# A written-out schedule of a fused attention and token-mixing kernel, laid out once more behind the first scores

## The chip, the cores and the metric

The kernel runs on one core of one Trainium2 chip. The metric is the device time of one execution in microseconds (us); the times of several executions are given as their median. The core has five engines that run side by side, each through its own instructions in a fixed order: PE (TensorE, matrix products; its weight loads are shown as PEld), DVE (VectorE), ACT (ScalarE), POOL (GpSimd) and SP (SyncE, which issues transfers). Transfers (DMAs) are issued by GpSimd, SP or ACT, and run in queues behind them on 16 DMA engines. An engine that needs another's result waits on a semaphore, and everything behind the waiting instruction on that engine waits too.

## What is computed

Two attentions one behind the other, for 8 batches, 8 heads, 576 tokens and a head size of 64, and then a token mixer over the 8 batches.

```python
def sm_attn(qq, kk, vv):
    s = scale * np.matmul(qq, kk.transpose(0, 1, 3, 2))
    s = s - np.max(s, axis=-1, keepdims=True)
    a = np.exp(s)
    a = a / (np.sum(a, axis=-1, keepdims=True) + 1e-09)
    return np.matmul(a, vv)
p_packed = sm_attn(p, k, v)               # 32 packed rows per head
out = sm_attn(q, p_packed, p_packed)      # 576 rows per head
...
x = out.transpose(0, 2, 1, 3).reshape(B, S, H * D)
wq = x @ w_q
wk = x @ w_k
W_tok = scale * np.einsum('bsd,btd->bst', wq, wk)
mixed = np.einsum('bst,btd->bsd', W_tok, x)
return (np.maximum(mixed, 0.0) @ w_out)
```

The inputs q, k and v are 8 x 8 x 576 x 64 in float32, the output is 8 x 576 x 512 in float32. The products run in bfloat16.

## The kernel before

The whole program is one list, the string ORDER, of some 520 items in a fixed order, with engine and banks written out. A loop at the end of the kernel takes the items one after the other and emits the instructions of each. An item reads `STEP.batch.part=banks@engine`: `PV.0.0=4,5` is the step PV of batch 0, part 0, with its result in PSUM banks 4 and 5, and `AE.0.2@A` is a step that runs on ACT (V is DVE, P is GpSimd; a store without a letter goes out by SP). Steps that are matrix products have no letter, since they run on PE. So the order of the list is the order of the instructions on each engine; between engines only the data and the buffers decide.

The steps of one batch b, in the order in which they depend on each other, with the lines under which the profile shows them:

- Loads: LD.k, LD.v, LD.q (L175, L172, L181; halves of q: LD.q7 and LD.r7, L178) by GpSimd's queue, cast from float32 to bfloat16 on the way. LD.O is the output weight, LD.N and LD.W are p and the two small weights (by ACT and SP).
- KT and QV (L236): transposes of k and of q on DVE, in blocks of 32 x 32.
- First attention: S1 (L281), scores of p with k; X1 (L292, ACT), their exponential; TE (L236, DVE), its transpose; PV (L314), the product with v, in which a column of ones gives the sum; RC (L318) and PP (L322) on DVE, the division; PT (L236, DVE), the transpose of the packed rows.
- Weights folded in: QK (L335), the packed rows times w_k and w_q; QKE, its copy out of PSUM (L127 on ACT, L131 on DVE); QD (L129, GpSimd), a second copy of a part.
- Second attention: S2 (L372), scores of q; X2 (L377, ACT), the exponential; RS (L393) and RR (L398) on DVE, sum and reciprocal (for batch 5 HA, L387, adds halves on GpSimd first); AM (L404, mostly GpSimd), the multiplication; AT (L413 and L418), the transpose on PE; AE (L127 or L131), its copy out of PSUM. Part 2 of S2, AM and AT is the last quarter of 256 elements, part 3 the four other token tiles (1,024 elements); in batches 0, 1 and 7 these are two parts, 0 and 1.
- Mixer: WKQ (L440, L445) and its copy WE; GM (L466) and GE; Y (L476) and YE (L483 on ACT, L485 on DVE); MX (L491) and MR (L497), the mixed rows; RL, RLF and RLR (L502 on ACT, L504 on DVE), the ReLU; OT (L539), the product with w_out, five tiles of 128 tokens (OT.b.4 for a pair of batches together); OE and OEF (L127 or L131), the copy out of PSUM; ST (L558, L560) and STF (L589), the stores. The last tile of batch 7 is done in halves: OH (L576), OEH and STH (L585).

WARM.n (L614) is a product of a constant buffer with itself, n times 128 columns, whose result nobody reads; it keeps PE at work while it would wait. HOLD.v7 (L571) is a tiny transfer by SP that reads v of batch 7: SP, whose stores stand behind it, goes no further until that load has landed.

The loads run in the order of the batches: k0, v0, q0, k1, k2, v1, q1, v2, q2, O, k3, v3, k4, q3, v4, q4, k5, v5, q5, k6, v6, q6, k7, and then the last ones. Input buffers are four deep, most others two or three, the result buffer o six (batch 6 writes where batch 0 lay, batch 7 where batch 1 lay). PE works on several batches at a time: while the first attention of one batch is on its way through ACT and DVE, PE does S2, WKQ or OT of an earlier one.

Of the kernel before, what the change touches and what calls it, by code (L numbers as in the profile page):

```python
# [13 lines left out]
LD.g0 LD.v0 LD.r0 LD.q0 LD.k1 NC.0@V PX.0@V NC.1@A PX.1@V SET.aff@P SET.idb@V SET.v3@P KT.0.0@V SET.mask@P  # L14
WC.1@P WC.0@P LD.k2 SET.v1@P LD.v1 SET.v2@P KT.0.1@V WARM.4=0 WARM.22.128=0 S1.0=0,1,2,3 X1.0.1@A TE.0.1@V
X1.0.0@A TE.0.0@V WARM.8=4 PV.0.0=4,5 PV.0.1 RC.0@V PP.0.0@V PP.0.1@V LD.q1 PT.0@V WARM.6=6 QK.0=6 QKE.0@A
QV.0.0@V QV.0.1@V QD.0@P WARM.4=7 S2.0.2=2,3 X2.0.2@A RS.0.2@V RR.0.2@V S2.0.0=0,1 LD.v2 S2.0.1=4,5 X2.0.0@A
RS.0.0@V RR.0.0@V X2.0.1@A RS.0.1@V RR.0.1@V AM.0.2@P WARM.6=7 AT.0.2=7 AE.0.2@A AM.0.0@P WARM.5=6 AT.0.0=6
KT.1.2@V AM.0.1@P WARM.3=2 AT.0.1=7 AE.0.1@A AE.0.0@V WKQ.0.0=2,3 WKQ.0.2 WE.0.0@A LD.q2 WKQ.0.1 KT.2.2@V
S1.1=0,1,4,5 WE.0.1@A GM.0=6 X1.1.0@A TE.1.0@V GE.0@A WARM.2=7 Y.0=2,3 YE.0@V S1.2=0,1,6,7 MR.0=2,3 X1.1.1@A  # L20
TE.1.1@V MX.0.0=4,5 X1.2.0@A LD.O PV.1.0=0,1 TE.2.0@V PV.1.1 X1.2.1@A TE.2.1@V RC.1@V LD.k3 PP.1.0@V PP.1.1@V
PT.1@V MX.0.1=6,7 QV.1.2@V RLR.0@A QK.1=2 QKE.1@V RL.0.0@A WARM.3=3 S2.1.2=4,5 S2.1.0=0,1 RL.0.1@A X2.1.2@A
RS.1.2@V RR.1.2@V S2.1.1=2,3 X2.1.0@A RS.1.0@V RR.1.0@V WARM.1=6 PV.2.0=6,7 PV.2.1 X2.1.1@A RS.1.1@V RC.2@V
LD.v3 QD.1@P AM.1.2@P AT.1.2=4 RR.1.1@V AM.1.0@P WARM.5=5 AT.1.0=5 AM.1.1@P LD.k4 PP.2.0@V AE.1.2@A PP.2.1@V
PT.2@V QK.2=4 AE.1.0@A QKE.2@A QD.2@P QV.2.2@V LD.q3 LD.v4 AT.1.1=0 AE.1.1@A WKQ.1.0=2,3 WKQ.1.2 WKQ.1.1
WE.1.0@V S2.2.2=6,7 WE.1.1@A X2.2.2@A S2.2.3=4,5 X2.2.3@A GM.1=1 OT.0.0=2,3 GE.1@V Y.1=6,7 OT.0.1 YE.1@A
RS.2.4@V OE.0.0@A MR.1=0,1 MX.1.1=4,5 RLR.1@A RR.2.4@V OT.0.2=6,7 LD.q4 OT.0.3 KT.3.2@V AM.2.3@P OE.0.1@V
RL.1.1@A S1.3=2,3,0,1 X1.3.0@A AM.2.2@P OT.1.4=4 TE.3.0@V LD.k5 AT.2.2=5 X1.3.1@A TE.3.1@V AT.2.3=2 AE.2.3@V
LD.v5 MX.1.0=6,7 AE.2.2@V PV.3.0=0,1 PV.3.1 OEF.1.4@A WKQ.2.0=2,3 WKQ.2.1 RC.3@V PP.3.1@V RL.1.0@A WKQ.2.2
WE.2.2@A OT.1.2=4,5 OT.1.3 PP.3.0@V PT.3@V QK.3=6 OE.1.1@A LD.q5 KT.4.2@V S1.4=0,1,2,3 GM.2=7 OT.1.0=4,5  # L30
X1.4.1@A LD.k6 GE.2@A QKE.3@V X1.4.0@A QV.3.2@V TE.4.1@V Y.2=2,3 YE.2@A S2.3.2=6,7 X2.3.2@A S2.3.3=0,1
X2.3.3@A MX.2.0=2,3 TE.4.0@V RL.2.0@A MR.2=6,7 RLR.2@V OT.1.1 MX.2.1=6,7 RL.2.1@A OE.1.0@A PV.4.0=0,1 QD.3@P
PV.4.1 RS.3.4@V RR.3.4@V LD.v6 AM.3.3@P AM.3.2@P RC.4@V OT.2.0=2,3 OT.2.1 LD.q6 OE.2.0@A PP.4.0@V PP.4.1@V
PT.4@V QK.4=6 AT.3.3=7 QV.4.2@V AT.3.2=0 AE.3.2@A LD.k7 S2.4.2=4,5 AE.3.3@V X2.4.2@A S2.4.3=2,3 X2.4.3@A
KT.5.2@V WKQ.3.0=0,1 WKQ.3.1 WKQ.3.2 RS.4.4@V RR.4.4@V QKE.4@A WE.3.2@A S1.5=4,5,2,3 X1.5.1@A LD.v7 TE.5.1@V
OT.2.2=6,7 AM.4.3@P QD.4@P AM.4.2@P GM.3=0 X1.5.0@A TE.5.0@V GE.3@A OT.2.3 Y.3=2,3 YE.3@V PV.5.0=4,5 PV.5.1
HOLD.v7 MR.3=0,1 RC.5@V PP.5.1@V OE.2.1@A MX.3.0=2,3 PP.5.0@V PT.5@V MX.3.1=6,7 RLR.3@A RL.3.0@A OT.3.4=0
RL.3.1@A AT.4.2=1 AE.4.2@A OEF.3.4@A QV.5.2@V AT.4.3=5 AE.4.3@V ST.1.4@P QK.5=4 QKE.5@V QD.5@P S2.5.2=2,3
X2.5.2@A KT.6.2@V S2.5.3=6,7 X2.5.3@A HA.5@P WKQ.4.0=0,1 WKQ.4.2 LD.q7 WKQ.4.1 WE.4.2@A OT.3.0=2,3
S1.6=4,5,6,7 X1.6.0@A GM.4=0 GE.4@V TE.6.0@V LD.r7 OT.3.1 X1.6.1@A TE.6.1@V Y.4=0,1 OE.3.0@A RS.5.4@V RR.5.4@V  # L40
PV.6.0=4,5 YE.4@A PV.6.1 MX.4.0=6,7 RC.6@V RL.4.0@A PP.6.0@V AM.5.3@P PP.6.1@V PT.6@V MX.4.1=2,3 AM.5.2@P
OT.3.2=0,1 OT.3.3 RL.4.1@A QK.6=4 QKE.6@A QV.6.2@V ST.2.1 S2.6.2=6,7 X2.6.2@A S2.6.3=2,3 ST.3.4 MR.4=4,5
# [5 lines left out]
OEF.5.4@A S2.7.1=6,7 ST.5.4 ST.1.0 GM.6=3 GE.6@V X2.7.1@A RS.7.1@V RR.7.1@V S2.7.2=0,1 X2.7.2@A S2.7.0=4,5
QK.7=2 X2.7.0@A RS.7.0@V RR.7.0@V Y.6=6,7 YE.6@A OT.5.2=0,1 MX.6.1=4,5 QKE.7@A MX.6.0=6,7 AM.7.1@P RS.7.2@V
RR.7.2@V MR.6=2,3 OT.5.3 RLR.6@V RL.6.0@V RL.6.1@A OE.5.1@A ST.4.1 AM.7.0@P OT.5.0=2,3 AM.7.2@P AT.7.0=4  # L50
AE.7.0@A AT.7.1=5 AE.7.1@V AT.7.2=6 AE.7.2@V OT.6.2=0,1 OEF.6.2@A QD.7@P WKQ.7.0=4,5 WKQ.7.2 WKQ.7.1 WE.7.0@A
WE.7.1@A STF.6.2 OT.6.0=6,7 OT.6.1 GM.7=0 OE.6.0@V OT.5.1 OE.5.0@V ST.5.1@P GE.7@A Y.7=4,5 OT.6.3 OEF.6.3@V
ST.6.0 STF.6.3 YE.7@A ST.5.0 MR.7=6,7 RLR.7@A MX.7.0=4,5 RLF.7.0.1@A RLF.7.0.0@V MX.7.1=2,3 RLF.7.1.0@A
OT.7.4=0 OEF.7.4@A ST.7.4 RLF.7.1.1@V OT.7.1=6 OEF.7.1@V OT.7.0=7 STF.7.1 OT.7.2=1 OEF.7.0@A OH.7.0=0 STF.7.0
OEF.7.2@A STF.7.2 OEH.7.0@V STH.7.0 OH.7.1=5 OEH.7.1@A STH.7.1@A
"""


# [589 lines left out]
```

## Time and profile before

| What | us |
|---|---|
| median of 3 executions | 104.16 |
| lowest and highest | 104.09 and 104.93 |
| the profiled execution | 104.06 |
| its span from the first instruction to the last | 102.2 |

The page of the profile gives for each engine how much of the span it was busy: PE 92.8 us (91%), DVE 73.5 us (72%), ACT 65.1 us (64%), GpSimd 53.3 us (52%). Its line of slices cuts the span into 40 equal parts of 2.56 us; GB/s counts the bytes that the DMA engines moved, where a load counts with its bfloat16 size. A row of the timeline gives start and length in us, the engine, the line, the operation, the output and the inputs by the program's names, the number of instructions merged into it (x2), and in brackets how long the engine had been idle and what ended that. Of products the length reaches to the end of the last one's tail, so that the next row of PE may begin before it.

### The profile page before, as it was taken

What the parts mean: (1) busy time and instruction counts of PE and PEld (TensorE: products, weight loads), DVE (VectorE), ACT (ScalarE), POOL (GpSimd) and SP (SyncE); (2) the same over time, 40 slices, a digit from 0 to 9 for tenths busy, and PEclk for the clock granted to TensorE, in tenths of its full rate; (3) what the DMA queues carried; (4) which work ended last, traced back from release to release, by engine and by line L of the source; (5) the groups of instructions that cost most, each with busy time, mean ns of one, the idle gap of its engine ahead of it and who ended that gap; (6) DMA issues with size and microseconds to landing.
All of it is one profiled execution on the core that took longest, in us unless ns stands there. A gap on an engine that the chain in (4) does not pass through costs nothing.

```text
span 102.2 us, 3594 instructions
## 1 busy us (share of the span) xinstructions
PE 92.8 (91%) x1536; PEld 54.6 (53%) x1536; DVE 73.5 (72%) x140; ACT 65.1 (64%) x111; POOL 53.3 (52%) x83
## 2 busy tenths in 40 slices
...
DMA  1999999999999999999999999999999999997894
GB/s 25 257 233 208 213 211 215 204 213 208 207 208 209 212 208 212 214 208 208 213 208 208 214 211 206 214 210 211 249 249 391 410 418 408 417 389 281 330 368 153
DMA packets 13567, 25.13 MB, mean 246 GB/s; under 512 B 1072, under 2 KB 6448, under 8 KB 13552
## 3 DMA queue, kind: packets, MB, share of 16 engines
...
q10 hardware_dynamic: 560, 0.52, 1.9%
...
HBM read 30.15 MB, written 9.44 MB: 387 GB/s over the span
## 4 chain that ended last, share of the span: by engine, by line
PE 50%; DMA 21%; DVE 8%; POOL 7%; ACT 7%; issue 3%; SPq 1%; POOLq 0%; DVEq 0%; ACTq 0%
PE ps L539 26%; DMA q_sb<-in_q_dram 13%; DMA o<-in_moe_w_q_dram 8%; PE ps L372 4%; POOL a L404 4%; PE ps L314 3%; ACT e1T L292 3%; PE ps L418 3%; PE ps L445 3%; DVE rs L393 2%; PE ps L440 2%; PE ps L466 2%; PE ps L281 2%; ACT e L377 1%; DVE qT L236 1%
## 5 line engine op out<-in xcount | busy, mean ns | idle before, releaser
L539 PE MATMUL ps<-wout,relu 128*128 128x512 bf16 x124 | 30.6, 380 | 0.0
L404 POOL TENSOR_TENSOR a<-e,rr 128x256 bf16<-128x256 f32 (+2 forms) x18 | 19.5, 1098 | 16.9 <-DVE rr L398 6.4
L614 PE MATMUL ps<-o 128*128 128x128 f32 (+3 forms) x76 | 19.3, 398 | 1.2 <-DVE o L134 1.2
L539 PEld LDWEIGHTS <-relu 128*128 128x128 bf16 x124 | 10.7, 98 | 11.7 <-issue 1.1
L127 ACT ACTIVATE o<-ps 128x1024 f32<-128x1024 f32 (+2 forms) x13 | 11.4, 878 | 5.4 <-PE ps L539 5.2
L614 PEld LDWEIGHTS ps<-o 128*128 128x128 f32 x76 | 11.2, 206 | 5.3 <-issue 3.6
L502 ACT ACTIVATE relu<-ps 128x1024 bf16<-128x1024 f32 (+1 forms) x14 | 12.9, 967 | 1.1 <-PE ps L491 1.1
L292 ACT ACTIVATE e1T<-ps 128x576 bf16<-128x576 f32 x16 | 9.8, 655 | 5.3 <-PE ps L281 4.7
L377 ACT ACTIVATE e<-ps 128x256 f32<-128x256 f32 (+2 forms) x19 | 11.2, 622 | 2.8 <-PE ps L372 2.6
L393 DVE TENSOR_REDUCE rs<-e 128x16 f32<-128x512 f32 (+2 forms) x13 | 10.9, 841 | 2.3 <-ACT e L377 2.2
L236 DVE STREAM_TRANSPOSE kT<-k_sb 128x1152 uint32<-128x1152 uint32 (+1 forms) x9 | 11.0, 1226 | 2.0 <-DMA k_sb<-in_k_dram 2.0
L172 POOL DMA_DIRECT2D v_sb<-in_v_dram x16 | 10.0, 629 | 4.6 <-DMA v_sb<-in_v_dram 1.4
L236 DVE STREAM_TRANSPOSE qT<-q_sb 128x1152 uint32<-128x1152 uint32 (+1 forms) x10 | 11.0, 1112 | 0.4 <-DMA q_sb<-in_q_dram 0.2
L131 DVE COPY o<-ps 128x1024 f32<-128x1024 f32 (+2 forms) x7 | 6.6, 958 | 5.0 <-PE ps L539 2.7
L236 DVE STREAM_TRANSPOSE e<-e1T 128x288 uint32<-128x288 uint32 x16 | 7.4, 469 | 2.5 <-ACT e1T L292 2.0
L127 ACT ACTIVATE aT<-ps 128x128 bf16<-128x128 f32 (+2 forms) x11 | 5.0, 465 | 5.7 <-PE ps L418 3.3
L314 PE MATMUL ps<-v_sb,e 64*64 64x192 bf16 x288 | 7.7, 245 | 0.8 <-DVE e L236 0.5
L127 ACT ACTIVATE wkq<-ps 128x448 bf16<-128x448 f32 (+1 forms) x10 | 7.2, 729 | 1.8 <-PE ps L445 1.7
L314 PEld LDWEIGHTS <-e 64*64 64x64 bf16 x288 | 6.0, 107 | 2.7 <-DVE e L236 2.0
L372 PEld LDWEIGHTS <-qT 64*128 64x128 bf16 x320 | 5.4, 94 | 2.8 <-DVE qT L236 1.8
L372 PE MATMUL ps<-ppT,qT 64*128 64x64 bf16 x320 | 6.6, 190 | 0.3 <-DVE qT L236 0.2
L445 PE MATMUL ps<-aT,pqk 128*128 128x256 bf16 (+1 forms) x48 | 6.8, 246 | 0.0
...
## 6 DMA issues: line engine op xcount, KB each, us to landing
...
```

The source lines that it names most:

```text
L127: nc.scalar.activation(o, i, COPY)
L172: nc.gpsimd.dma_start(v_bufs[b % NL][halves(i), 0:7:2], src)
L236: nc.vector.transpose(o, i)
L292: nc.scalar.activation(e1T[:, x], T["s1", b][x].rearrange("a c m -> a m c"), EXP, scale=scale)
L314: nc.tensor.matmul(T["pv", b][halves(cc), i], lhsT, rhs, start=n == 0, stop=n == R - 1, skip_group_check=True)
L372: nc.tensor.matmul(ps[:, y, t - t0, i], lhsT, rhs, start=e == 0, stop=e == 1)
L377: nc.scalar.activation(e2[:, t0:t1].rearrange("a t (i y n) -> a y (t i) n", i=2, y=2), T["s2", b, c].rearrange("a y t i n -> a y (t i) n") ...
L393: nc.vector.tensor_reduce(rs[:, t0 * H:t1 * H], src, axis=AX, op=ADD)
L404: e.tensor_tensor(a2[:, t0:t1].rearrange("a t i (u l) -> a (t i u) l", l=L), e2v(b, c), T["rr", b][:, t0 * H:t1 * H].to_broadcast((P, (t1 ...
L502: nc.scalar.activation(o, i, RELU)
L539: nc.tensor.matmul(ps, lhsT, wout[:, j, :], start=j == 0, stop=j == NJ - 1)
L614: nc.tensor.matmul(bank(int(bk), [w]), warm[:, 0:P], rhs, start=True, stop=True)
```

## The change

Nothing but the string ORDER is changed, from its second line on. Up to the first scores (S1.0) only LD.k2 and setup steps of GpSimd and KT.0.1 change place; the steps behind them are laid out once more: their order, the banks of their results, and for 28 steps the engine. Every load, product and store of the old list stands in the new one; the WARM items differ (69 units of 128 columns before, 79 after). Of the loads, q7 comes ahead of v7; it was between v7 and r7.

For the steps that the prediction speaks of, by engine, with the old order under the minus sign and the new one under the plus sign:

```diff
 PE, from the first wait for q of batch 1
-QK.1 WARM.3 S2.1.2 S2.1.0 S2.1.1 WARM.1 PV.2.0 PV.2.1 AT.1.2 WARM.5 AT.1.0 QK.2 AT.1.1 WKQ.1.0 WKQ.1.2 WKQ.1.1 S2.2.2 S2.2.3 GM.1
-OT.0.0 Y.1 OT.0.1 MR.1 MX.1.1 OT.0.2 OT.0.3 S1.3 OT.1.4 AT.2.2 AT.2.3 MX.1.0 PV.3.0 PV.3.1 WKQ.2.0 WKQ.2.1 WKQ.2.2 OT.1.2 OT.1.3
-QK.3 S1.4 GM.2 OT.1.0 Y.2 S2.3.2 S2.3.3 MX.2.0 MR.2 OT.1.1 MX.2.1 PV.4.0 PV.4.1 OT.2.0 OT.2.1 QK.4 AT.3.3 AT.3.2 S2.4.2 S2.4.3
+WARM.1 QK.1 WARM.7 S2.1.2 S2.1.0 S2.1.1 WARM.4 PV.2.0 PV.2.1 AT.1.2 WARM.4 AT.1.0 QK.2 WKQ.1.0 WKQ.1.2 AT.1.1 S2.2.2 S2.2.3 WKQ.1.1
+OT.0.2 OT.0.3 GM.1 OT.0.0 OT.0.1 Y.1 S1.3 MR.1 AT.2.2 AT.2.3 MX.1.0 MX.1.1 PV.3.0 PV.3.1 WKQ.2.0 WKQ.2.2 WKQ.2.1 OT.1.2 OT.1.3
+GM.2 QK.3 S1.4 Y.2 OT.1.4 MX.2.1 S2.3.2 S2.3.3 OT.1.0 MR.2 MX.2.0 PV.4.0 PV.4.1 OT.1.1 OT.2.0 OT.2.1 QK.4 AT.3.3 AT.3.2 S2.4.2 S2.4.3
...
 PE, batch 5
-PV.5.0 PV.5.1 MR.3 MX.3.0 MX.3.1 OT.3.4 AT.4.2 AT.4.3 QK.5 S2.5.2 S2.5.3 WKQ.4.0 WKQ.4.2 WKQ.4.1 OT.3.0 S1.6 GM.4 OT.3.1 Y.4 PV.6.0
+PV.5.0 PV.5.1 AT.4.2 MR.3 MX.3.0 MX.3.1 OT.3.4 AT.4.3 S2.5.2 S2.5.3 WKQ.4.0 WKQ.4.1 WKQ.4.2 OT.3.0 S1.6 GM.4 OT.3.1 QK.5 Y.4 PV.6.0
...
 PE, the end
-AT.7.0 AT.7.1 AT.7.2 OT.6.2 WKQ.7.0 WKQ.7.2 WKQ.7.1 OT.6.0 OT.6.1 GM.7 OT.5.1 Y.7 OT.6.3 MR.7 MX.7.0 MX.7.1 OT.7.4 OT.7.1 OT.7.0 OT.7.2 OH.7.0 OH.7.1
+AT.7.1 AT.7.2 OT.5.1 AT.7.0 OT.6.2 WKQ.7.0 WKQ.7.1 WKQ.7.2 OT.6.0 GM.7 OT.6.1 Y.7 OT.6.3 MR.7 MX.7.0 MX.7.1 OT.7.4 OT.7.2 OT.7.1 OT.7.0 OH.7.1 OH.7.0
 DVE, batches 1 to 2
-RS.1.0 RR.1.0 RS.1.1 RC.2 RR.1.1 PP.2.0 PP.2.1 PT.2 QV.2.2 WE.1.0 GE.1 RS.2.4 RR.2.4 KT.3.2 OE.0.1 TE.3.0
+RS.1.0 RR.1.0 RS.1.1 RC.2 PP.2.1 PP.2.0 PT.2 RR.1.1 AE.1.0 QV.2.2 RS.2.4 RR.2.4 KT.3.2 YE.1 RLR.1 TE.3.1
 DVE, batches 3 to 5
-PT.3 KT.4.2 QKE.3 QV.3.2 TE.4.1 TE.4.0 RLR.2 RS.3.4 RR.3.4 RC.4 PP.4.0 PP.4.1 PT.4 QV.4.2 AE.3.3 KT.5.2 RS.4.4 RR.4.4
-TE.5.1 TE.5.0 YE.3 RC.5 PP.5.1 PP.5.0 PT.5 QV.5.2 AE.4.3 QKE.5 KT.6.2
+PT.3 KT.4.2 GE.2 QKE.3 QV.3.2 TE.4.0 RL.2.1 TE.4.1 RS.3.4 RR.3.4 RC.4 PP.4.0 PP.4.1 PT.4 QV.4.2 QKE.4 AE.3.3 KT.5.2 RS.4.4 RR.4.4
+TE.5.0 TE.5.1 YE.3 RC.5 PP.5.0 PP.5.1 QV.5.2 PT.5 AE.4.3 KT.6.2
 DVE, batch 7
-AM.6.3 TE.7.1 TE.7.0 QV.7.1 AE.6.3 QV.7.0 RC.7 PP.7.0 PP.7.1 PT.7 RL.5.0 GE.6
+AM.6.3 TE.7.0 GE.5 TE.7.1 QV.7.1 AE.6.3 AE.6.2 RC.7 QV.7.0 PP.7.0 PP.7.1 PT.7 RL.5.0 GE.6
 GpSimd, from the AM steps of batch 2, and its stores
-LD.q4 AM.2.3 AM.2.2 LD.k5
+LD.q4 AM.2.2 AM.2.3 LD.k5
...
-LD.q6 LD.k7 LD.v7 AM.4.3 QD.4 AM.4.2 ST.1.4 QD.5 HA.5 LD.q7 LD.r7 AM.5.3 AM.5.2 ST.1.1 ST.0.1 ST.3.0 AM.6.2 QD.6 AM.7.1 AM.7.0 AM.7.2 QD.7 ST.5.1
+LD.q6 LD.k7 LD.q7 AM.4.2 QD.4 AM.4.3 LD.v7 HA.5 ST.1.4 LD.r7 AM.5.2 AM.5.3 ST.3.0 QD.5 ST.3.4 ST.0.1 QD.6 ST.1.1 AM.6.2 AM.7.1 AM.7.2 AM.7.0 QD.7
 SP, its stores
-HOLD.v7 ST.2.1 ST.3.4 ST.4.0 ST.2.0 ST.0.0 ST.3.1 ST.5.4 ST.1.0 ST.4.1 STF.6.2 ST.6.0 STF.6.3 ST.5.0 ST.7.4 STF.7.1 STF.7.0 STF.7.2 STH.7.0
+HOLD.v7 ST.4.0 ST.0.0 ST.1.0 ST.4.1 ST.5.4 ST.2.0 ST.5.1 ST.2.1 STF.6.2 ST.5.0 ST.3.1 ST.6.0 STF.6.3 ST.7.4 STF.7.2 STF.7.1 STF.7.0 STH.7.0
```

So ST.3.4 goes from SP's queue to GpSimd's, and ST.5.1 from GpSimd's to SP's: GpSimd issues five stores in either list. The steps that change their engine and that the prediction names are AE.1.0, GE.2, QKE.4, GE.5 and AE.6.2, all from ACT to DVE.

More of the change, by code (lines that the diff above doesn't have):

```diff
@@ L13 @@
 LD.N0@A LD.N1@S SET.warm@V SET.v0@V SET.aT0@V SET.aT1@V SET.aT2@V SET.idf@V LD.W0@A LD.W1@S SET.tab@A LD.h0
[L14 to L42, printed above, removed]
@@ L48 @@
[L48 to L52, printed above, removed]
@@ L53 @@
[L53 to L55 removed]
+LD.g0 LD.v0 LD.r0 LD.q0 LD.k1 NC.0@V PX.0@V NC.1@A PX.1@V SET.aff@P SET.idb@V KT.0.0@V KT.0.1@V SET.v2@P
+WARM.4=0 WARM.22.128=0 S1.0=0,1,2,3 X1.0.0@A LD.k2 X1.0.1@A TE.0.0@V TE.0.1@V WARM.8=4 PV.0.0=4,5 PV.0.1
+RC.0@V SET.mask@P PP.0.1@V PP.0.0@V WC.0@P PT.0@V SET.v1@P LD.v1 QV.0.0@V LD.q1 WC.1@P LD.v2 WARM.6=6 QK.0=6
@@ new lines @@
+QV.0.1@V WARM.4=7 S2.0.2=0,1 QKE.0@V QD.0@P X2.0.2@A RS.0.2@V RR.0.2@V S2.0.0=2,3 X2.0.0@A RS.0.0@V RR.0.0@V
+S2.0.1=4,5 X2.0.1@A AM.0.2@P RS.0.1@V RR.0.1@V AM.0.0@P WARM.12=7 AT.0.0=7 AT.0.2=6 AE.0.0@A KT.1.2@V AM.0.1@P
+WARM.2=0 S1.1=0,1,2,3 AT.0.1=7 AE.0.1@V AE.0.2@A X1.1.0@A X1.1.1@A WKQ.0.0=4,5 WKQ.0.1 WKQ.0.2 WE.0.0@A LD.q2
+SET.v3@P KT.2.2@V WARM.3=6 S1.2=0,1,6,7 WE.0.1@A GM.0=2 TE.1.0@V X1.2.0@A TE.1.1@V GE.0@V WARM.2=3 Y.0=4,5
+TE.2.0@V PV.1.0=2,3 PV.1.1 LD.O LD.k3 YE.0@V X1.2.1@A MR.0=0,1 RLR.0@A MX.0.1=6,7 MX.0.0=4,5 TE.2.1@V RC.1@V
@@ new lines @@
+LD.v3 PP.1.0@V RL.0.1@A PP.1.1@V PT.1@V WARM.1=0 QK.1=0 QKE.1@A QV.1.2@V WARM.7=1 S2.1.2=2,3 RL.0.0@A X2.1.2@A
+S2.1.0=6,7 X2.1.0@A S2.1.1=0,1 LD.k4 RS.1.2@V RR.1.2@V AM.1.2@P QD.1@P WARM.4=4 PV.2.0=4,5 PV.2.1 X2.1.1@A
+AT.1.2=2 AE.1.2@A RS.1.0@V RR.1.0@V AM.1.0@P WARM.4=3 AT.1.0=3 RS.1.1@V RC.2@V PP.2.1@V PP.2.0@V PT.2@V QK.2=2
+RR.1.1@V QKE.2@A AE.1.0@V WKQ.1.0=6,7 WKQ.1.2 AM.1.1@P WE.1.0@A AT.1.1=0 AE.1.1@A QV.2.2@V S2.2.2=4,5 X2.2.2@A
+S2.2.3=2,3 X2.2.3@A RS.2.4@V LD.q3 RR.2.4@V WKQ.1.1 WE.1.1@A KT.3.2@V OT.0.2=0,1 OT.0.3 GM.1=6 OT.0.0=4,5
@@ new lines @@
+LD.v4 QD.2@P LD.q4 OE.0.1@A OT.0.1 GE.1@A Y.1=2,3 YE.1@V S1.3=0,1,6,7 OE.0.0@A MR.1=2,3 AM.2.2@P AT.2.2=4
+AM.2.3@P AT.2.3=5 LD.k5 RLR.1@V X1.3.1@A TE.3.1@V X1.3.0@A TE.3.0@V MX.1.0=2,3 RL.1.0@A MX.1.1=6,7 RL.1.1@A
+PV.3.0=0,1 AE.2.3@V AE.2.2@V PV.3.1 RC.3@V PP.3.0@V WKQ.2.0=4,5 WKQ.2.2 WKQ.2.1 WE.2.2@A OT.1.2=2,3 OT.1.3
+GM.2=0 PP.3.1@V PT.3@V KT.4.2@V QK.3=1 S1.4=6,7,4,5 OE.1.1@A GE.2@V Y.2=2,3 X1.4.0@A OT.1.4=0 YE.2@A QKE.3@V
+LD.v5 X1.4.1@A QV.3.2@V MX.2.1=6,7 OEF.1.4@A S2.3.2=2,3 X2.3.2@A TE.4.0@V RL.2.1@V S2.3.3=4,5 X2.3.3@A
```

29 lines of the change are left out of this document (24 added, 5 removed).

## The prediction

> **What bounds the kernel now.** I read the page first: the span line, the slices, and the chain of waits.
>
> ```profile
> span 102.2 us, 3594 instructions
> ...
> DMA  1999999999999999999999999999999999997894
> GB/s 25 257 233 208 213 211 215 204 213 208 207 208 209 212 208 212 214 208 208 213 208 208 214 211 206 214 210 211 249 249 391 410 418 408 417 389 281 330 368 153
> ...
> PE 50%; DMA 21%; DVE 8%; POOL 7%; ACT 7%; issue 3%; SPq 1%; POOLq 0%; DVEq 0%; ACTq 0%
> ```
>
> The GB/s line has two plateaus: about 210 up to slice 28 (some 72 us), the loads, and about 410 from slice 31, the stores. The DMA line stays at 9 almost to the end, so the loads arrive at a fixed pace, one batch about every 8.5 us (72 us for eight batches, and a remainder). PE carries half of the chain. Next I asked for the busy time by stage, cut at the starts of S2.1, S1.3, S1.5, PV.6 and S2.7:
>
> ```profile
> 28.28:39.73 11.45, 10.99 (x193) 6.44 (x193) 8.70 (x17) 7.48 (x14) 7.89 (x11) 1.00 1.17 209
> 39.73:57.05 17.32, 16.33 (x337) 9.54 (x337) 14.41 (x25) 13.23 (x22) 10.48 (x15) 1.00 1.15 211
> 57.05:68.00 10.95, 10.43 (x234) 6.04 (x236) 8.75 (x17) 9.96 (x17) 6.89 (x10) 1.00 1.13 210
> 68.00:82.00 14.00, 13.96 (x266) 8.51 (x268) 13.69 (x23) 12.05 (x20) 6.13 (x7) 1.00 1.10 298
> 82.00:98.40 16.40, 16.31 (x175) 8.65 (x174) 10.22 (x19) 10.44 (x22) 3.52 (x5) 1.00 0.94 373
> ```
>
> The columns are the stretch, its length, then busy time of PE, PEld, DVE, ACT and POOL, granted clock, DMA share, GB/s. PE idles 0.46 + 0.99 + 0.52 + 0.04 + 0.09 = 2.1 us in 70 us. So PE's own work sets the end, the loads set when each batch may start, and DVE, 98% busy from 68 to 82 us, stands between them. What a new order can win is little; what it can lose is new waits.
>
> **The change, part by part.** The loads keep their order but for q7, now ahead of v7 and r7, and every one is still issued several microseconds ahead of its turn; the page's flat 210 GB/s says that an earlier issue buys nothing. So I keep all arrival times. The matrix products are the same; only the WARM fillers grow. I follow PE from the first wait for a load to the end, each step starting when its engine and its inputs are ready.
>
> *To S1.3.* WARM.7 stands ahead of S2.1 where WARM.3 stood.
>
> ```profile
> 27.12 0.91 PE L614 MATMUL ps<-o 128*128 128x384 f32 x2
> ...
> 28.28 0.78 PE L372 MATMUL ps<-ppT,qT 64*128 64x64 bf16 x40 [0.25 <-DVE qT L236]
> ...
> 31.10 0.25 DVE L398 RECIPROCAL rr<-rs 128x16 f32<-128x16 f32 x1
> ...
> 32.38 1.38 DVE L236 STREAM_TRANSPOSE qT<-q_sb 128x1152 uint32<-128x1152 uint32 x1 [0.25 <-DMA q_sb<-in_q_dram]
> ...
> 34.31 0.78 PE L372 MATMUL ps<-ppT,qT 64*128 64x64 bf16 x40
> ...
> 39.73 0.49 PE L281 MATMUL ps<-kT,pT 32*32 32x288 bf16 x32
> ```
>
> Three units take 0.7 to 0.9 us, seven 1.5 to 2.1 (7/3 of them), from about 27.0: S2.1 starts at 28.6, some 0.3 late. Then RR.1.1 (0.25) and AE.1.0 on DVE (some 0.4, half as wide as the aT copy of 0.69 at 55.02 below) go ahead of QV.2, which moves from 32.38 to 33.0 and ends at 34.4. S2.2 starts at 34.45 against 34.31; the whole late start but 0.15 falls into the wait that stood ahead of it. KT.3 and S1.3 follow at about 39.85. But MR.1 and MX.1.1, which PE did before S1.3, now lie behind it, so 0.4 us of work is owed.
>
> *S1.3 to PV.3.* OT.1.4 leaves the place ahead of AT.2, and AM.2.2 goes ahead of AM.2.3.
>
> ```profile
> 37.50 0.38 PE L491 MATMUL ps<-wkq,y 64*128 64x512 bf16 x2
> ...
> 38.39 2.48 POOL L404 TENSOR_TENSOR a<-e,rr 128x1024 bf16<-128x1024 f32 x2 [2.08 <-DVE rr L398]
> ...
> 40.15 1.04 PE L539 MATMUL ps<-wout,rem 128*128 128x512 bf16 x4
> ...
> 42.14 0.94 PE L314 MATMUL ps<-v_sb,e 64*64 64x192 bf16 x36
> ```
>
> The pair of AM.2 ends at 38.39 + 2.48 = 40.87, whichever goes first; the large one, which AT.2.3 needs, is now the second. PE is through S1.3 and MR.1 at 40.35 and waits 0.6 us for it where it had OT.1.4 to do. It does both MX.1 and reaches PV.3 at 42.2, as before, owing OT.1.4 (0.9: its four products take 1.04 with the last one's tail).
>
> *To S1.5.* Four steps of DVE change place.
>
> ```profile
> 44.24 1.34 DVE L236 STREAM_TRANSPOSE kT<-k_sb 128x1152 uint32<-128x1152 uint32 x1
> ...
> 46.15 0.42 DVE L131 CAST pqk<-ps 128x256 bf16<-128x256 f32 x1 [0.57 <-PE ps L335]
> ...
> 46.49 1.37 DVE L236 STREAM_TRANSPOSE qT<-q_sb 128x1152 uint32<-128x1152 uint32 x1
> ...
> 48.01 1.01 PE L372 MATMUL ps<-ppT,qT 64*128 64x64 bf16 x40
> ...
> 50.52 0.94 PE L314 MATMUL ps<-v_sb,e 64*64 64x192 bf16 x36
> ...
> 55.02 0.69 DVE L131 COPY aT<-ps 128x1024 bf16<-128x1024 bf16 x1 [0.57 <-PE ps L418]
> ...
> 55.62 1.37 DVE L236 STREAM_TRANSPOSE kT<-k_sb 128x1152 uint32<-128x1152 uint32 x1
> ...
> 57.05 0.48 PE L281 MATMUL ps<-kT,pT 32*32 32x288 bf16 x32 [0.32 <-DVE kT L236]
> ```
>
> GE.2 (some 0.3: half of the elements of QKE's 0.42) comes to DVE ahead of QKE.3 and QV.3: QV.3 starts at 46.87, ends at 48.25, and S2.3 starts at 48.3, 0.3 late. OT.1.4 is made up ahead of it, OT.1.0 behind it. PV.4 is on time at 50.5, because PE had nothing to spare there either way; what is owed is OT.1.1 (0.9), which stood ahead of PV.4 and now follows it. That puts QK.4 and AT.3.3 0.4 to 0.5 us later, and QKE.4 (0.42), now on DVE, stands ahead of AE.3.3: of the 0.57 us that DVE waited before AE.3.3 nothing is left. AE.3.3 starts at 55.35 and KT.5 at 56.0, so S1.5 starts at 57.45: **0.4 us late**.
>
> *To S2.7.* PT.5 goes behind QV.5, and QK.5 from the place ahead of S2.5 to one ahead of Y.4.
>
> ```profile
> 61.72 1.34 DVE L236 STREAM_TRANSPOSE qT<-q_sb 128x1152 uint32<-128x1152 uint32 x1
> ...
> 63.11 0.78 PE L372 MATMUL ps<-ppT,qT 64*128 64x64 bf16 x40
> ...
> 67.97 0.94 PE L314 MATMUL ps<-v_sb,e 64*64 64x192 bf16 x36 [0.47 <-DVE e L236]
> ...
> 69.22 1.91 POOL L404 TENSOR_TENSOR a<-e,rr 128x1024 bf16<-128x1024 f32 x1 [1.54 <-DVE rec L318]
> ...
> 70.04 1.34 DVE L236 STREAM_TRANSPOSE qT<-q_sb 128x1152 uint32<-128x1152 uint32 x1
> ...
> 80.89 0.31 DVE L236 STREAM_TRANSPOSE ppT<-pp 128x128 uint32<-128x128 uint32 x1
> ```
>
> S2.5 needs both transposes: 63.11 + 0.4 carried + the part of PT's 0.31 (the ppT row) that isn't overlapped (0.1 to 0.3) makes 63.6. QK.5 (0.3) then fills the hole ahead of PV.6, where PE idled 0.47; so the lag is back at 0.4 there. From PV.6 on both orders keep PE full: 0.3 to 0.4 us late at S2.7. On DVE, GE.5 and AE.6.2 (0.3 each) come in, and QV.7.0 falls between RC.7 and PP.7: PT.7 ends at about 82.1 instead of 81.2, just ahead of S2.7 at 82.3. Its price is nothing with that cover, up to 0.5 without.
>
> [...] In the trace AM.5.3 took 1.91 us from 69.22, while DVE's transpose ran beside it from 70.04 for 1.1 us. [...]
>
> *The end.* Behind S2.7 stand the same steps. OT.5.1 goes ahead of AT.7.0, and OT.6.1 behind GM.7; WKQ.7 then waits for AE.7.0 and MX.7.1 for OE.6.0, each by 0 to 0.1 us.
>
> ```profile
> 97.32 1.04 PE L576 MATMUL ps<-wout,relu 128*128 128x256 bf16 x8
> ...
> 98.81 0.64 ACTq L585 DMA_DIRECT2D out_dram<-o  x1
> ...
> out_dram<-o ACTq DMA_DIRECT2D x1, 128.0 KB, 2.5
> ```
>
> PE ended at 98.36; it will end at 98.36 + 0.35 + 0.1 = 98.8, and the last store goes out at 99.25. By the view of DMA issues its landing took 2.5 us, behind the other stores. In slices 37 and 38 the DMA moved 281 and 330 GB/s instead of some 415: 0.56 MB, 1.35 us of the engines, went unused since SP's next store wasn't ready. Now old stores (ST.2.1, ST.3.1) are kept for that stretch, so the queue is shorter at the end: I take 2.35 us. The end moves by 0.45 - 0.15 = **0.3 us**.
>
> SP's own part: HOLD.v7 keeps its stores back until v7 has landed, now behind q7, so 1.4 us later (288 KB at 210 GB/s), and ST.2.1 and ST.3.1, ready long before, are queued behind ST.5.1, which waits for OE.5.1.
>
> ```profile
> 75.52 0.62 SPq L571 DMA_DIRECT2D touch<-v_sb  x1
> ...
> 86.19 1.02 ACT L127 ACTIVATE o<-ps 128x1024 f32<-128x1024 f32 x1 [0.16 <-PE ps L539]
> ```
>
> Ahead of that lie four stores of GpSimd's and six of SP's, 18 times 256 KB, 4.7 MB: at 415 GB/s 11.4 us. The loads end at about 78 us, so the DMA has work until 89, and ST.5.1 goes out at 87.6. Cover gone (the stores quicker, OE.5.1 late), it would cost what the gap is, 1 us at most, of engine time that isn't short.
>
> GpSimd's own part: ST.3.4 comes to its queue and ST.5.1 leaves it, so it issues five stores as before, four of them now between r7 and AM.6.2 instead of three. That one more issue is hidden: GpSimd idled 2.64 us before that step; it costs 0.6 if that wait is gone.
>
> ```profile
> 76.18 1.58 POOL L404 TENSOR_TENSOR a<-e,rr 128x256 bf16<-128x256 f32 x1 [2.64 <-DVE rr L398]
> ```
>
> The profiled run took 104.06 us (span 102.2 and 1.86 around it), the median is 104.16. 104.06 + 0.3 = 104.36, and 0.1 for the median: **104.4 us**.
>
> **Rivals.** *DVE becomes the pacer.* Each of KT.5, QV.5, PT.6 and KT.7 starts late, and DVE has no idle time to give it back from 68 us (13.69 of 14.00 us busy). If PE's order has no work in front of those steps, the 0.6 us at AT.2.3, 0.4 at S1.5, 0.25 at S2.5 and 0.3 at S2.7 add up instead of covering each other: 104.16 + 1.55 = 105.7. It decides if DVE's chain from RS.3.4 to KT.5 is over 0.6 us late, more than PE's owed OT can fill. Against it: before 57 us PE's owed work fills waits.
>
> *The stalls go and nothing takes their place.* Of the 2.1 us that PE idled, the holes ahead of S1.5 (0.32) and PV.6 (0.47) and the 0.46 before S1.3 are touched by the change. All gone: 104.16 - 1.25 = 102.9. The store stream would allow it, having 1.35 us unused. Against it: the waits counted above.
>
> *Nothing changes.* PE's lag is all absorbed where it waits for a load anyway, and GpSimd issues as many stores as it did: 104.1 to 104.2.
>
> **How the numbers follow.** The forecast has 0.5, no change 0.17, DVE as pacer 0.2, fewer stalls 0.13. About 1% (1.04 us) can be told from no change. The range of 103.2 to 105.8 takes in the ends of the unknown terms (0.4 without WARM's and PT.7's, 0.5 with the port) and the slower rival, and leaves out most of the faster one. Faster by over 1% (below 103.1): 0.12. Slower (over 105.2): 0.05 from the forecast's upper end and most of the pacer, 0.23. Within: 0.65.
>
> **What would show it.** Right: S2.2 and S1.3 within 0.2 us of before, a new wait of PE for AM ahead of AT.2.3, S2.5 waiting for ppT instead of qT, S1.5 at 57.3 to 57.6, PE's last product ending at 98.6 to 99.0, and slices 37 and 38 fuller. Wrong: a load landing late, PE waiting over 0.5 us behind 68 us, or SP's stores still landing in a queue after PE's end.

## The result, and the profile after

| | before | after |
|---|---|---|
| median of 14 executions each, on the same chip | 104.19 us | 104.86 us |
| lowest to highest | 103.91 to 104.93 | 104.50 to 105.83 |
| the profiled execution | 104.06 us | 104.97 us |
| its span | 102.2 us | 103.1 us |

The ratio is 1.0067, with a 95% interval of 1.0043 to 1.0091: slower by 0.7%, which lies within the 1% that the prediction counted as no change. The forecast of 104.4 us was 0.5 us short, the range held the time. As the rest shows, the reason given for the loss was the wrong one. Ratios and intervals leave out executions in a slower state of the chip, and of all kernels below only the one with fewer, wider WARM products had any (3 of 12), which its median still counts.

The page of the kernel after, with the span, the DMA slices, the instruction packets and the engines' shares of the chain of waits:

```profile
span 103.1 us, 3582 instructions
...
DMA  1999999999999999999999999999999999899991
GB/s 25 248 232 206 214 214 207 208 213 204 212 208 210 209 210 210 214 207 210 212 208 210 214 207 209 212 210 212 225 300 406 412 420 376 356 387 373 354 333 48
...
q8 instruction: 12, 0.20, 0.7%
...
PE 66%; DVE 13%; DMA 7%; ACT 3%; POOL 3%; issue 3%; DVEq 0%; POOLq 0%; ACTq 0%
```

The two plateaus are unchanged. The store plateau is different: before, it had one hole of two slices (281 and 330 GB/s, slices 37 and 38); now it has shallow dents in slices 34, 35 and 37 to 39, and a last slice of 48 GB/s. That last slice is the result in small: the core waits for a DMA stream that hardly moves anything. The q8 line is one that I had passed over: 12 transfers that no line of the kernel issues, 0.20 MB in all, some 16 KB each.

Where the 0.9 us of the profiled execution went is seen by following PE. Its last step and the last issues of the kernel after, from the timeline:

```profile
97.34 1.04 PE L576 MATMUL ps<-wout,relu 128*128 128x256 bf16 x8
...
98.83 0.54 SPq L585 DMA_DIRECT2D out_dram<-o  x1
```

PE ended at 97.34 + 1.04 = 98.38 us, against 98.36 before, and the last store went out at 98.83, against 98.81. So nothing at all was lost up to the last issue; the whole loss lies between that issue and the last landing. The view of DMA activity from 98.9 to 103 us, in slices of 0.1 us, first for the kernel before and then for the kernel after:

```profile
DMA  9995899999999999996000000000000000000000
GB/s 420 360 360 180 300 420 400 360 360 360 380 330 350 330 340 320 360 350 220 20 0 0 0 0 0 0 0 0 0 0 0 0 0 0 0 0 0 0 0 0
```

```profile
DMA  9999999998999999997300000000000000000000
GB/s 380 400 380 380 320 340 400 440 380 340 400 320 350 350 340 330 370 360 270 100 30 20 20 30 20 20 30 20 20 0 0 0 0 0 0 0 0 0 0 0
```

Before, the stream stops at once, after 19 slices. After, it falls off at the same place and then runs on for nine slices at 20 to 30 GB/s. All 16 engines together move some 350 to 400, so 20 to 30 GB/s is about one engine (a sixteenth of them is 22 to 25). Fifteen engines were done at the time of before; one was 0.9 us behind, and the span ran on until the last store's sixteenth landing at 102.22 us (in the table below).

The trace records sixteen landings for each store, as many as there are engines, but not which engine each was. Taken as one for each engine they fit the tail: nine slices of 0.1 us above, and 0.85 us between the last two landings. From those records, for stores in the order of SP's queue after, the last of all at the end (us):

```
                      after                        before
store          15th engine   16th   gap     15th engine   16th   gap
STF.6.2              93.47  93.72  0.25           94.61  94.74  0.13
ST.5.0               94.96  95.94  0.98           97.76  97.89  0.13
ST.6.0               97.45  98.39  0.94           95.87  96.00  0.13
STF.6.3              98.09  99.00  0.91           96.51  96.64  0.13
ST.7.4               98.80  99.63  0.83           98.42  98.53  0.11
last to land        101.37 102.22  0.85          101.25 101.27  0.02
```

In the kernel after, the gap opens at ST.5.0 and never closes. In between, at 92.90 us, lies one packet of q8: 16,384 bytes that took 945 ns on one engine. By their times, packets of 441 and 271 ns follow on the same engine. All sixteen landings say how much that engine lost. STF.6.2 landed on thirteen engines by 92.37 us and on three at 93.09 to 93.72; ST.5.0 landed on twelve by 93.62, on three at 94.38 to 94.96, and on one at 95.94. In the order of landing, fifteen engines needed 1.2 to 1.3 us from the one to the other, and one of the thirteen level ones needed some 3.7, so it lost 2.4 us. The packet and the two long ones behind it are some 1.3 us of that; the rest no row explains. The gap to the 15th engine is smaller than 2.4 us because three others trailed too.

A like packet stands in the trace of before, at 92.28 us and 879 ns long, and it left no gap. What differs is what the engines had to do at that time, seen in the DMA activity from 86 to 96 us, in slices of 0.25 us, before and then after:

```profile
DMA  9999999999999999999999865743179999703999
```

```profile
DMA  8999886647999989999979998999898978698999
```

Before, the engines run partly empty from slice 23 to 30 (91.5 to 93.5 us), around the packet, and almost wholly at slices 36 and 37 (94.75 to 95.25 us), behind it. By the packet records, some seven of the 16 engines had nothing to do at 92.28 us; the packet starts as a part of a store ends, and no store packet starts as it ends. So its engine seems to have been out of work, and the packet delayed nothing. After, those holes are filled but for dents, and an earlier one has opened at slices 5 to 10 (87.0 to 88.5 us), ahead of the packet. The earlier hole is SP standing at ST.5.1:

```profile
83.11 5.35 SPq L560 DMA_DIRECT2D out_dram<-o  x3
```

Of these three stores the first went out at 83.11, the second, ST.5.1, only at 87.27 us, behind its wait for OE.5.1, and the third at 87.85.

### The profile page after: what moved, and what is told of

Its sections match the earlier page's. It is cut to its first block, busy times and chain, and to the rows that moved or that the text cites. A ratio compares the mean times of both kernels' runs of the same rounds, so it can differ in the third digit from the quotient of the medians.

```text
span 103.1 us, 3582 instructions
## 1 busy us (share of the span) xinstructions
PE 93.3 (90%) x1525; PEld 55.1 (53%) x1538; DVE 73.7 (71%) x142; ACT 65.4 (63%) x109; POOL 53.1 (51%) x83
## 4 chain that ended last, share of the span: by engine, by line
PE 66%; DVE 13%; DMA 7%; ACT 3%; POOL 3%; issue 3%; DVEq 0%; POOLq 0%; ACTq 0%
PE ps L539 26%; PE ps L614 10%; DMA k_sb<-in_k_dram 7%; PE ps L314 5%; PE ps L372 5%; PE ps L418 3%; PE ps L445 3%; PE ps L281 3%; DVE qT L236 3%; POOL a L404 2%; PE ps L491 2%; PE ps L440 2%; PE ps L335 2%; DVE kT L236 2%; DVE pp L322 2%
## 5 line engine op out<-in xcount | busy, mean ns | idle before, releaser
L539 PE MATMUL ps<-wout,relu 128*128 128x512 bf16 x114 | 29.1, 380 | 0.7 <-issue 0.3
L614 PE MATMUL ps<-o 128*128 128x128 f32 (+3 forms) x78 | 21.8, 422 | 1.2 <-DVE o L134 1.2
L127 ACT ACTIVATE o<-ps 128x1024 f32<-128x1024 f32 (+2 forms) x14 | 12.4, 887 | 6.8 <-PE ps L539 6.4
L502 ACT ACTIVATE relu<-ps 128x1024 bf16<-128x1024 f32 (+1 forms) x13 | 12.1, 954 | 0.6 <-PE ps L491 0.6
L131 DVE COPY o<-ps 128x1024 f32<-128x1024 f32 (+2 forms) x6 | 5.4, 912 | 4.0 <-PE ps L539 1.9
```

Source lines behind the costliest of these rows:

```text
L127: nc.scalar.activation(o, i, COPY)
L502: nc.scalar.activation(o, i, RELU)
L539: nc.tensor.matmul(ps, lhsT, wout[:, j, :], start=j == 0, stop=j == NJ - 1)
L614: nc.tensor.matmul(bank(int(bk), [w]), warm[:, 0:P], rhs, start=True, stop=True)
```

## The experiments

Three theories. **F**: an instruction packet on one DMA engine costs its length if the engines are full from there to the end, and nothing if they run empty behind it; the new store order moved the hole from behind the packet to ahead of it. **S**: the stream lost the time in which SP stood at ST.5.1, and with it the last landing. **C**: the order of the products and of DVE costs the time, as predicted. Every experiment was timed in five rounds beside the kernel before.

**The new order with the old stores, and the old order with the new stores.** First, the change but for the stores: SP and GpSimd issue them in the old order.

```diff
-HOLD.v7 ST.4.0 ST.0.0 ST.1.0 ST.4.1 ST.5.4 ST.2.0 ST.5.1 ST.2.1 STF.6.2 ST.5.0 ST.3.1 ST.6.0 STF.6.3 ST.7.4 STF.7.2 STF.7.1 STF.7.0 STH.7.0
+HOLD.v7 ST.2.1 ST.3.4 ST.4.0 ST.2.0 ST.0.0 ST.3.1 ST.5.4 ST.1.0 ST.4.1 STF.6.2 ST.6.0 STF.6.3 ST.5.0 ST.7.4 STF.7.1 STF.7.0 STF.7.2 STH.7.0
```

> The changed kernel with the stores of before: SP's queue has its old order, and GpSimd issues ST.1.1, ST.0.1, ST.3.0 and ST.5.1 at its old places. Theory F (the stores' fill of the DMA engines meets a 16 KB instruction fetch at about 93 us, which puts one of the 16 engines 0.95 us behind until the end): PE's last product ends at 98.4 as now, the last store lands at about 101.3 instead of 102.2, time 104.0 to 104.3. Rival S (SP stands at ST.5.1 from 83.7 to 87.3 and the engines idle at 87 to 89 us): the same, 104.1 to 104.4. Rival C (the order of the compute steps costs the 0.7 us): 104.7 to 105.0.

Measured: 104.75 us, ratio 1.005 (1.0018 to 1.0082). That is the time that C forecast, but not for C's reason: PE ended at 98.28 us. The engines were level at the end (gap 0.02), and it was slow because ST.6.0 and the last three stores stand in SP's queue in an order in which the new steps no longer finish. ST.6.0 went out at 93.32 instead of 92.19 us, and the last store at 99.34 instead of 98.81. The reverse (the old steps with SP's and GpSimd's new store order):

> The kernel before with the stores of the changed one, in SP's order and on GpSimd's queue; the compute steps and the loads (v7 ahead of q7) as before. F and S: 104.7 to 105.0, the last store landing 0.6 to 0.9 us later than before. C: 104.1 to 104.3.

Measured: 105.98 us, ratio 1.0165 (1.014 to 1.0191); ST.5.0 waits for OE.5.0 until 93.67 us and the last store goes out at 100.42. All forecasts missed this time. Neither run can say which part of the change costs what: an order of stores fits one order of steps, and mixing them makes waits of its own.

**Moving the packet.** More, narrower WARM products in the kernel after were to bring the packets forward; fewer, wider ones in the kernel before to put them off.

```diff
-WARM.8=4 ... WARM.6=6 ... WARM.4=7 ... WARM.12=7 ... WARM.7=1 ... WARM.4=4 ... WARM.4=3
+WARM.5.128=4 ... WARM.4.128=6 ... WARM.3.128=7 ... WARM.8.128=7 ... WARM.5.128=1 ... WARM.3.128=4 ... WARM.3.128=3
```

> The changed kernel; seven WARM items behind S1.0 are made of products of 128 columns instead of 512 and have fewer columns, so that PE has some 76 instructions more in the same time. If PE's instructions are fetched by their count (one packet about every 256), the fetch that came at 92.9 us comes some 4 us earlier (19 instructions per us there), at 88 to 89 us, where the DMA engines idle. F: 104.1 to 104.4, and no engine behind the others from 95 us. S and C: 104.7 to 105.0, as the changed kernel. If the packet stays at 93 us the run tells nothing of F.

Measured: 105.59 us, ratio 1.0141 (1.0111 to 1.0171). The packet came at 89.89 us, where the other engines were idle, and the engines were level at the end, but PE itself was 1.3 us later at S2.1 and 2.4 us at its end. So every forecast of the time was missed, and the time does not say what the packet was worth. The other way, in the kernel before:

```diff
-WARM.22.128=0
+WARM.22=0
```

> The kernel before; WARM.22, ahead of the first scores, is made of products of 512 columns instead of 128, 64 instructions of PE fewer for the same columns. If the fetch goes by count, the one at 92.3 us comes some 3.4 us later, at 95 to 96 us, where the stores keep all engines full. F: 104.7 to 105.1, one engine 0.9 us behind the others at the end. S and C: 104.1 to 104.3, as before. If the packet stays at 92 to 93 us the run tells nothing of F.

Measured: 104.39 us, ratio 1.0005 (0.998 to 1.0029), with runs from 103.71 to 105.71. F's forecast of the time was missed. The execution that was profiled is the one of 105.71 us, and its landings look like F: the packet came at 97.91 us; the gap was 0.03 us at STF.6.3, 2.00 at ST.5.0 and still 1.02 at the last landing. The last store went out at 99.48 us, 0.67 later than before, which adds to the time. Where the packet fell in the other eleven executions is not recorded, so it stays open why most were as quick as the kernel before.

**Giving SP work while it stands.** One, and then two of the old stores go ahead of ST.5.1 in the kernel after; nothing else is changed.

```diff
-... ST.5.4 ST.2.0 ST.5.1 ST.2.1 STF.6.2 ST.5.0 ST.3.1 ST.6.0 ...
+... ST.5.4 ST.2.0 ST.2.1 ST.5.1 STF.6.2 ST.5.0 ST.3.1 ST.6.0 ...
```

> The kernel after with one old store, ST.2.1, moved ahead of ST.5.1 in SP's order, so that SP has work for the engines while it waits for OE.5.1. Theory F (one DMA engine is put 0.9 us behind by an instruction packet that falls where all engines are full, and every later store lands with that engine): the idle at 87 to 89 us is filled and returns at 94 to 97, engines still apart at the end, 104.5 to 104.9. Theory S (the store stream lost what SP stood still at ST.5.1): 104.2 to 104.4. Theory C (the compute order costs it): 104.8 as after.

Measured: 104.57 us, ratio 1.0048 (1.0025 to 1.007). The packet came at 91.9 us, ST.5.0 again opened a gap (1.08 us between its 15th and 16th engine), and at the last landing 0.58 us of it was left. The time is in F's range.

```diff
-... ST.5.4 ST.2.0 ST.5.1 ST.2.1 STF.6.2 ST.5.0 ST.3.1 ST.6.0 ...
+... ST.5.4 ST.2.0 ST.2.1 ST.3.1 ST.5.1 STF.6.2 ST.5.0 ST.6.0 ...
```

> The kernel after with ST.2.1 and ST.3.1 ahead of ST.5.1 in SP's order, so that no old store is left for the last 10 us and the engines run empty for over 1 us around 93 us, where the instruction packet falls. Theory F: the engines come out of that stretch level (15th and 16th engine within 0.2 us of each other at every later landing), the last landing falls from 102.2 to about 101.2, 103.8 to 104.2. Theory S (lost engine time decides): the idle of 87 to 89 us comes back at 93, nothing won in sum, 104.5 to 104.9. Theory C: 104.8.

Measured: 104.00 us, ratio 0.9986 (0.9968 to 1.0003). Two stores in one queue take back the whole loss, with every product and every step of the change in place: C falls. The DMA activity of this kernel from 86 to 96 us, and from 98.9 us on:

```profile
DMA  9999999999999999999799999999653522999998
```

```profile
DMA  9997999999999999982000000000000000000000
```

The hole is back, at slices 29 to 34 (93.0 to 94.5 us), right behind the packet, which lies at 92.90 us as in the kernel after and took as long there (948 ns, then 440 and 267). The stream ends after 19 slices with no tail of one engine; the last store landed at 101.19 us on the last engine and 101.18 on the 15th. Here a lag was made up: the slowest engine landed ST.5.0 at 95.96 us, as late as in the kernel after (95.94), and first and last engine were 1.06 us apart at ST.6.0 and 0.15 at the last store. In the kernel after it was 2.14 and still 1.09. The idle engine time from 84 to 100 us, summed over slices of 1 us, was 1.28 us, against 1.10 in the kernel after and 1.35 in the kernel before. S falls with that: the kernel after lost the least engine time of the three and ended last.

**A packet made on purpose.** The kernel before gets one more transfer that nothing reads, 15.5 KB in 31 rows, meant to lie on one engine alone.

```diff
+    def XT(b, eng, bk):
+        nc.scalar.dma_start(xtra[0:31], moe_w_out[0:31, 0:128])
...
-OEF.7.4@A ST.7.4
+OEF.7.4@A XT.7@A ST.7.4
```

> The kernel before, with one more transfer of 16 KB that nothing reads, on one DMA engine alone (31 rows of an input to an unused tile), issued by ACT behind OEF.7.4 at about 95.6 us, where ACT idles 1.1 us and all DMA engines are full. It adds 0.4% of the bytes of the last 10 us, 0.04 us if spread over 16 engines. Theory F: the engine that carries it is 0.6 to 1.0 us behind at the last landings, and the time is 104.8 to 105.2. Rival (the amount and the issue times of the stores decide): 104.2 to 104.3, landings level within 0.2 us.

Measured: 104.88 us, ratio 1.0065 (1.0043 to 1.0087), the loss of the change itself. The DMA activity of this kernel, from 98.9 us:

```profile
DMA  9999959899999999999940000000000000000000
GB/s 380 380 360 360 400 180 340 340 360 400 440 360 320 340 350 340 340 320 360 330 160 10 30 20 30 20 20 30 0 0 0 0 0 0 0 0 0 0 0 0
...
xtra<-in_moe_w_out_dram ACTq DMA_DIRECT2D x1, 15.5 KB
```

The tail of one engine is there again, seven slices at 10 to 30 GB/s. The last landings stand 0.70 us apart; another 0.15 us comes from the last store's issue, at 98.96 us. The same transfer some 6 us earlier, ahead of the hole:

```diff
-WE.7.1@A STF.6.2
+WE.7.1@A XT.7@A STF.6.2
```

> The same transfer of 16 KB on one engine, issued by ACT behind WE.7.1 at about 90 us, ahead of the stretch at 92 to 95 us where the kernel before leaves the DMA engines idle for 1.3 us in sum. Theory F: the lag is made up in that stretch, 104.1 to 104.4, engines level at the last landings. Rival: as the late one, whatever that is.

Measured: 104.14 us, ratio 0.9997 (0.9977 to 1.0018), gap 0.02 us. The same bytes on one engine cost 0.65 us or nothing. The 31 packets show why. Late, they ran from 96.17 to 98.53 us, and the last eight came 0.18 us apart, with room for a store's packet of 0.159 us in each gap. Early, they ran from 90.62 to 91.98 us, and the last 13 followed each other directly: their engine had no store left. By the store packets between the others, it was one of the first engines to land STF.6.2 (91.58 to 94.69 us over the 16). So in this pair the bytes cost nothing (gap 0.02 us) on an engine that was about to run empty. That a lag already there is made up is shown by the two stores early, not by this pair.

**Without the last packet.** In the kernel after, and in the kernel before as its control, 31 of the WARM products are left out (they add nothing to the result).

```diff
-WARM.22.128=0 ... WARM.8=4 ... WARM.6=6 ... WARM.12=7 ... WARM.2=0 ... WARM.2=3 ... WARM.1=0 ... WARM.7=1
+... WARM.4=6 ... WARM.4=7 ... WARM.4=1
```

> The kernel after, its stores and its order as they are, with 31 fewer warming products on PE in the first 28 us (62 PE instructions with their weight loads), so that the last of the 12 instruction packets, which is asked for some 64 PE instructions ahead of the end, should not be needed or fall at 97 us or later. Theory F: without that packet at 93 us the engines stay level (15th and 16th engine within 0.2 us at the last landings), the last landing is at about 101.3 and the time 104.0 to 104.2. If the packet only moves to 97 to 98 us, a lag remains: 104.4 to 105. Theory S (idle of 87 to 89 us): 104.8 as after. If PE's clock falls for want of the products, all is later by what S2.1 is late.

> The kernel before with the same 31 products left out of its first 28 us. Theory F: its packet fell into idle engine time anyway, so nothing is won: 104.1 to 104.3. If the products are worth time by themselves, both kernels move alike.

Measured: 105.76 us, ratio 1.0162 (1.0133 to 1.0191), and 106.64 us, ratio 1.0226 (1.0184 to 1.0268). Both expected times were missed: PE was 1.7 and 2.5 us later at its end, because the products are worth more than I thought (last section). The case that the first expectation named for this came out in it: S2.1 was 1.65 us late and PE's end 1.67. But the last packet was gone; either kernel has 11, the last at 87.74 and 89.98 us, where the engines run partly empty. The page of the first has one q8 transfer less:

```profile
q8 instruction: 11, 0.18, 0.6%
```

And in it, with the stores of the kernel after unchanged, the gap at the last landing was 0.02 us. So the time from PE's end to the last landing can be compared across kernels. It is free of PE's lateness, but not of a last issue that comes late. So the kernel after with the old stores stands apart, and the two other kernels whose last issue came late (before with the new stores, and with fewer, wider WARM) are left out:

```
kernel                                PE's end  last landing  between   gap
before                                   98.36        101.27     2.91  0.02
after                                    98.38        102.22     3.84  0.85
after, more and narrower WARM           100.77        103.69     2.92  0.01
after, one store early                   98.50        101.99     3.49  0.58
after, two stores early                  98.28        101.19     2.91  0.01
before, 16 KB on one engine, late        98.52        102.14     3.62  0.70
before, 16 KB on one engine, early       98.30        101.22     2.92  0.02
after, 31 WARM fewer (no last packet)   100.05        102.97     2.92  0.02
before, 31 WARM fewer (no last packet)  100.89        103.81     2.92  0.02
after, old stores                        98.28        101.88     3.60  0.02  (last issue 1.06 behind PE)
```

Where the last issue was not late, level engines give 2.91 to 2.92 us whatever else was changed; each gap adds about its own length.

## Why the prediction was right in its verdict and wrong in its reason

**The steps on PE.** The forecast of each start against what the trace of the kernel after shows (us):

```
                     forecast   after    before
S2.1                    28.6    28.48    28.28
S2.2                    34.45   34.32    34.31
S1.3                    39.85   39.69    39.73
PV.3                    42.2    42.10    42.14
S2.3                    48.3    48.15    48.01
PV.4                    50.5    50.32    50.52
AE.3.3 (DVE)            55.35   54.96    55.02
S1.5                    57.45   56.99    57.05
S2.5                    63.6    63.06    63.11
S2.7                    82.3    81.97    81.94
PE's end                98.8    98.38    98.36
last store's issue      99.25   98.83    98.81
its time to landing      2.35    3.39     2.46
```

*To S1.3 and PV.3: right.* S2.1 was 0.2 us late and S2.2 on time: the wait ahead of it took the delay, as argued. PE now waits for AM ahead of AT.2.3, 0.32 us where 0.6 was said, and reaches PV.3 on time:

```profile
40.93 0.62 PE L418 MATMUL ps<-idb,a 128*128 128x128 bf16 x8 [0.32 <-POOL a L404]
...
42.10 0.94 PE L314 MATMUL ps<-v_sb,e 64*64 64x192 bf16 x36
```

*To S1.5: this step failed, by 0.46 us.* I made AT.3.3 late with QK.4, behind the owed OT.1.1. QK.4 was indeed 0.46 late. But a row of before that I did not use says what AT.3.3 waits for. Before, and then after:

```profile
53.43 0.41 PE L335 MATMUL ps<-wqk,ppT 64*64 64x128 bf16 x8
54.29 0.62 PE L418 MATMUL ps<-idb,a 128*128 128x128 bf16 x8 [0.44 <-POOL a L404]
```

```profile
53.89 0.41 PE L335 MATMUL ps<-wqk,ppT 64*64 64x128 bf16 x8
54.30 0.62 PE L418 MATMUL ps<-idb,a 128*128 128x128 bf16 x8
```

AT.3.3 waited 0.44 us for GpSimd's AM.3.3, which started at 52.32 us before and at 52.34 after. The owed product went into that wait and filled it: no bracket is left in the second row. On DVE, QKE.4 went in the same way into the 0.57 us that DVE had idled ahead of AE.3.3:

```profile
54.41 0.42 DVE L131 CAST pqk<-ps 128x256 bf16<-128x256 f32 x1
54.96 0.69 DVE L131 COPY aT<-ps 128x1024 bf16<-128x1024 bf16 x1
55.57 1.37 DVE L236 STREAM_TRANSPOSE kT<-k_sb 128x1152 uint32<-128x1152 uint32 x1
...
61.44 1.37 DVE L236 STREAM_TRANSPOSE qT<-q_sb 128x1152 uint32<-128x1152 uint32 x1
62.73 0.27 DVE L236 STREAM_TRANSPOSE ppT<-pp 128x128 uint32<-128x128 uint32 x1
```

*To S2.7: right but for what it inherited.* With S1.5 on time, QV.5 started 0.28 us earlier than before, since PT.5 no longer stood ahead of it, and PT.5 behind it ended at 62.73 + 0.27 = 63.00. S2.5 came at 63.06. The view of stages, from PV.6 to S2.7 and from there to the end, shows no new wait of size; the trace of after lacks 13 of the 1,538 product records, all of OT steps, and those account for part of the lower PE sum of the first row:

```profile
67.99:82.00 14.01, 13.65 (x260) 8.44 (x266) 13.54 (x24) 12.36 (x20) 7.03 (x10) 1.00 1.10 295
82.00:98.40 16.40, 16.24 (x173) 8.48 (x174) 10.19 (x18) 10.95 (x22) 2.90 (x4) 1.00 0.96 377
```

*The 0.5 us "with the port" in the range* is shown by no run: the AM steps of 1,024 elements on GpSimd took 1.90 to 1.91 us in the kernel after, with DVE's transposes of q and k beside them for 0.41 us (AM.4.3) to 1.33 us (AM.5.3), and the same in the kernel before, and PE ended at 98.38 us against 98.36.

*The end: wrong in both halves.* "The queue is shorter at the end" was wrong by its own bytes: old stores kept for the hole are stores that did not go out earlier, so the hole only moved, from 91.5 to 87.0 us, and the engines' idle time stayed 1.1 to 1.35 us. The landing took 3.39 us instead of the 2.35 taken. Of the 0.15 us that a shorter queue was to save, no run shows anything: from the last issue to the last landing it was 2.46 us in the kernel before and 2.47 with two stores early, both with level engines. And that SP's stand at ST.5.1 "would cost what the gap is, 1 us at most, of engine time that isn't short" had the place right (SP out at 87.27, forecast 87.6) and the price wrong. The cover it counted on, work for the DMA until 89 us, had dents from 87.0 on, since the engines do not finish together: ST.2.0, the last store ahead of the stand, landed on the first engine at 87.06 us and on the last at 90.64. In sum no more engine time was idle than before; what was lost is the idle stretch around and behind the packet, in which it costs nothing or is made up. The price, 0.85 us by the gap in the profile, does not appear in the means over 16 engines on which I argued, since one engine 0.9 us behind is 0.06 us of their mean.

So the sum was +0.45 - 0.15 = +0.3 us; measured were +0.02 up to the last issue and +0.93 behind it, which is the 0.9 us between the two profiled executions, and 0.67 us between the medians. That the forecast came near is luck: two errors of opposite sign.

*The signs and the rivals.* Of the signs named for being right, S2.2 and S1.3 near their old places, PE's new wait ahead of AT.2.3 and the fuller slices 37 and 38 came; S1.5 and PE's end lay outside their ranges. DVE did not become the pacer, and the stalls did not go. "Nothing changes" was right for PE, which ended 0.02 us from before, though the lag went into waits for GpSimd and DVE as well as for loads; it was wrong for the time. None of the cases named the mechanism that decided; what I had listed as wrong if seen, "SP's stores still landing in a queue after PE's end", is close to what happened.

The kernel with two stores early, at 104.00 us, is the best of the study. It repairs the change; that it beats the kernel before cannot be said, since its interval reaches 1.0003.
